# A searched table of due times replaced by ten rounds of forward and backward list scheduling

## The chip, the cores and the metric

The kernel runs on one core of a Trainium2 chip. The core has five engines that run side by side, each through its own list of instructions in order: TensorE (PE, matrix products; PEld is its weight load), VectorE (DVE), ScalarE (ACT), GpSimd (POOL) and SyncE (SP, which here only issues DMAs). They meet through semaphores: an instruction that waits holds back everything behind it on its own engine. The metric is the time of one execution in microseconds (us) on the device.

## The reference

Two layers, each an attention without softmax over positions and a gated MLP, on x of 2048 rows by 512, both with the same weights. Cut to what is computed:

```python
def A(x):                                  # 32 heads of 16
    q, k, v = split(x @ wqkv)
    pq, pk = q @ w_phi, k @ w_phi          # per head, 16 x 16
    phi_q = [softmax(pq), softmax(-pq)]    # over 16 features
    phi_k = [softmax(pk), softmax(-pk)]
    kv, z = phi_k.T @ v, sum_s phi_k       # per head, over all 2048 rows
    return (phi_q @ kv / (phi_q @ z + 1e-6)) @ wo

def B(x):
    gate, up = x @ W_gate, x @ W_up        # 512 -> 1376
    return (relu(gate) * up) @ W_down      # 1376 -> 512

for layer in range(2):
    x = x + A(layernorm(x))
    x = x + B(layernorm(x))
```

## The kernel before

The 2048 rows are 16 tiles of 128. All of x stays on the chip; the weights are loaded once. The work of a layer, per tile unless said otherwise:

- **Keys.** Mean and variance of the row (`stats`, L524, and `aggr`, L525, VectorE), the root (`ln`, L530, and `rstd`, L532, ScalarE), the scaled row (`xnA`, L535, VectorE), its transpose by a DMA that SyncE issues (L512; tiles 0 to 3 of layer one go over TensorE instead, L515). Then the products `K` (L555) and `V` (L561), four matmuls each; two exponentials of K (`ek`, L558, ScalarE), their sums (`sk`, L566, VectorE), the reciprocals (`lnk`, L569, and `rk`, L571, ScalarE), the normalised features (`phi`, L575: on GpSimd for tiles 0 to 14 of layer one, half on GpSimd and half on VectorE for tile 15, nearly all on VectorE in layer two), the copy of V (`vext`, L479, ScalarE), and the product `kvz` (L590), summed over all tiles in three PSUM banks.
- **Queries**, for four tiles at a time and a quarter of the features: the product `Q` (L627) and two exponentials `Eq` (L631, ScalarE). The weight for it is wq times w_phi, made from wq transposed out of DRAM by DMA (L487, folded at L500).
- **Read-out.** When all keys of the layer are summed and copied (`R`, L607, L614, VectorE), each tile has three packs of products `erq` (L645), two copies of each by ScalarE (L652, `DS` for the denominators and `N`), a chain on VectorE (`m`, `den`, `rden`, `w`, `pr`, `o`, L658 to L670), a transpose `oT` (DMA, or TensorE and ScalarE for the first two tiles of a layer), the product `proj` with wo (L674) and the sum into x (`resA`, L678, VectorE).
- **MLP**, in blocks of one to four tiles: statistics again, centring (`xc`, L693), a transpose `xnTB`, the products `G` and `Up` (L717), a relu and a copy by ScalarE (`rg`, L729, and `ru`, L732), their product (`hT`, L735, VectorE), the products `down` (L753), and the sum into x (`resB`, L760, VectorE). In layer two the finished tile is stored.

Nobody writes the order of these operations by hand. The code makes a list of 2,072 operations, each with its engine, its buffers, an assumed occupancy and latency, and a due time. The function `plan` then walks through the list: it keeps a clock for each engine and, at each step, takes the engine that can go first and on it, of the operations that could start within 1 ns of that moment, the one with the earliest due time. It models the few PSUM and SBUF buffers, a lock between VectorE and GpSimd (`port`), and a queue of DMAs. The order it returns is the order in which each engine's instructions are emitted. So the due times set the order on all five engines, and nothing else in the program depends on them. In the kernel before, `arrange` reads them from a table of 2,072 numbers, `DUE`, that stands in the file.

Of the kernel before, what the change touches and what calls it, by code (L numbers as in the profile page):

```python
# [148 lines left out]
def arrange(ops):  # L149
    taker = {b: o for o in ops for b in o.takes}  # L150
    last = {}
    for o in ops:
        for b in o.takes:
            if b.pool.fifo:
                if b.pool in last:
                    o.follow.append(last[b.pool])
                last[b.pool] = o
    assert len(ops) == len(DUE)
    for n, o in enumerate(ops):
        o.n, o.due = n, DUE[n]  # L160
        o.follow += {taker[b] for b in o.uses} - set(o.deps) - set(o.follow)
        for d in o.deps:
            d.then.append(o)
        for d in o.follow:
            d.behind.append(o)
    return plan(ops)
# [39 lines left out]
class K:  # L206
# [7 lines left out]
)  # L214
PHI = ["POOL"] * 15 + ["BOTH"]
BLOCKS = ((1, 1, 2, 4, 4, 2, 2), (1, 1, 2, 4, 4, 2, 1, 1))

DUE = (  # L220
    12838, 22903, 21957, 14591, 13091, 13645, 15535, 64723, 20066, 21946, 22404, 37433, 28497, 23438, 37063, 39628,
    28785, 29551, 44842, 28330, 24305, 34896, 63622, 64383, 20084, 27070, 12367, 25403, 16122, 20963, 16400, 20414,
    28622, 14745, 13296, 0, 20852, 19738, 11034, 1902, 20892, 15574, 21335, 14487, 15440, 22432, 23645, 18853, 17105,
    22553, 28873, 19773, 26092, 25340, 25787, 23828, 13120, 23528, 21785, 24083, 23090, 21952, 20538, 24815, 23457,
    25970, 23550, 31010, 25099, 23275, 18650, 19003, 26038, 17503, 25082, 25647, 15810, 16800, 15591, 12341, 14834,
    14960, 22006, 26736, 27644, 31701, 20249, 19795, 19482, 28729, 28028, 25143, 23422, 23168, 21986, 20764, 21010,
    18380, 22535, 26069, 26704, 26760, 27662, 26937, 23439, 25716, 25111, 22983, 25319, 23584, 22831, 20905, 24972,
    20900, 23792, 31557, 26979, 24090, 26712, 27328, 29633, 36593, 23721, 21790, 27888, 29989, 28308, 24211, 23690,
    16282, 27043, 28746, 63959, 20753, 24108, 22204, 20506, 28938, 31501, 16952, 23241, 24872, 26922, 26823, 26681,
    23442, 21284, 21898, 21956, 23204, 34727, 23722, 25793, 25045, 24516, 28101, 34925, 27683, 29170, 28253, 28875,  # L230
    30193, 28228, 27230, 20124, 19920, 25218, 34824, 20364, 26494, 23600, 22279, 25188, 32338, 24418, 23597, 25625,
    24807, 22909, 26881, 23790, 23537, 27214, 30398, 27170, 29691, 24862, 29838, 30880, 31272, 31170, 24090, 19394,
    24355, 27559, 28096, 28185, 27041, 16432, 19783, 20871, 21413, 25680, 24329, 22590, 23232, 28648, 34644, 25165,
    27573, 28614, 28868, 26952, 25768, 33460, 18665, 20698, 17926, 25363, 24420, 41432, 26543, 26946, 21970, 28607,
    28989, 25096, 31074, 29971, 29937, 25959, 28788, 30567, 21366, 23689, 25468, 26088, 25065, 28026, 32472, 33442,
    31477, 34059, 28202, 31806, 26064, 29854, 28369, 27149, 33755, 29216, 28180, 39321, 29625, 29410, 29759, 29949,
    30883, 29890, 21203, 25098, 24304, 21581, 23455, 24475, 31469, 24994, 27083, 22812, 27946, 25205, 43875, 15559,
    25460, 23347, 27182, 23482, 28342, 27010, 22914, 29784, 25417, 28800, 29241, 25959, 25485, 27617, 28609, 37268,
    25605, 25139, 29044, 33664, 26596, 31241, 22317, 27365, 31505, 25855, 27240, 29739, 29776, 24515, 29496, 27055,
    48013, 29990, 29010, 24738, 30465, 29653, 26383, 27215, 24572, 27986, 31540, 32648, 30111, 27816, 16563, 19041,  # L240
    9479, 23219, 25309, 26030, 26104, 29231, 28181, 27070, 27672, 28078, 20393, 17154, 22122, 19588, 25751, 27454,
    22139, 24767, 25652, 32015, 26913, 31404, 30354, 28037, 29609, 34266, 27656, 28104, 28466, 28450, 31160, 30434,
    26952, 30569, 30612, 27119, 30871, 33399, 32067, 34072, 29086, 34212, 32746, 34162, 34371, 32689, 31635, 34109,
    30452, 37680, 37561, 41767, 41154, 37244, 39966, 41520, 39034, 39714, 38939, 40611, 36774, 37121, 40048, 41493,
    40952, 40145, 35401, 33634, 20214, 31855, 33609, 22183, 27678, 29428, 20348, 24850, 30274, 21932, 28328, 31959,
    27444, 26877, 28606, 28895, 24453, 29898, 25480, 23901, 30133, 28911, 24856, 31383, 32228, 24030, 31506, 28199,
    32754, 31472, 31274, 25668, 31210, 30983, 31349, 33831, 34333, 33193, 27960, 30503, 30056, 29661, 29544, 32065,
    30471, 32168, 24516, 30101, 33395, 31799, 26788, 23122, 25970, 29642, 30372, 35556, 29123, 28474, 26295, 29799,
    27380, 29844, 29799, 26910, 29198, 22079, 25297, 29171, 32706, 31300, 31881, 33230, 30935, 33150, 30287, 28298,
    32473, 30062, 29409, 29680, 30383, 30476, 33342, 32180, 31884, 29485, 29126, 29096, 33750, 23466, 26796, 33931,  # L250
    30478, 30721, 31905, 30348, 31049, 32479, 30642, 29053, 27874, 29598, 32147, 30603, 25630, 31540, 36090, 27634,
    32676, 33746, 30843, 29434, 32969, 31529, 32324, 31334, 31554, 34777, 34212, 32334, 38155, 32871, 30137, 29960,
    27864, 27548, 35055, 34867, 30643, 30379, 32482, 31185, 33273, 31190, 30927, 29246, 28310, 31240, 38117, 29632,
    31893, 34024, 31843, 26885, 32603, 33936, 31021, 29366, 34535, 31275, 26896, 30743, 31011, 31248, 32477, 23864,
    32959, 25458, 29236, 31247, 34346, 26139, 33228, 38199, 31455, 38062, 40710, 31812, 38651, 40364, 31420, 41742,
    34183, 28837, 32652, 31832, 34298, 28327, 30341, 29521, 35561, 33294, 32671, 38050, 36251, 32854, 38333, 38562,
    31856, 42479, 47161, 29669, 28655, 35988, 32438, 29020, 34168, 29930, 35502, 32080, 31770, 41960, 44038, 32126,
    40768, 41997, 32384, 40042, 36094, 30450, 23249, 35852, 30672, 27603, 33194, 29517, 25790, 23365, 31969, 35815,
    34051, 32276, 32677, 33417, 32709, 35178, 32911, 41034, 32059, 37788, 34836, 33304, 30046, 24875, 36165, 42408,
    33005, 31288, 32714, 33009, 32695, 34948, 32971, 33157, 31154, 31289, 32065, 32216, 35950, 28322, 32715, 31866,  # L260
    34581, 38918, 33400, 32312, 34615, 33401, 30952, 29225, 33240, 29997, 32764, 35036, 31619, 31739, 35561, 28264,
    32661, 27143, 25474, 38415, 34139, 37169, 35696, 33672, 36588, 36260, 33373, 35663, 35325, 37087, 39060, 37213,
    40757, 38129, 39949, 32093, 28904, 44808, 26281, 23717, 30612, 29287, 28651, 31781, 29154, 30604, 30605, 27971,
    19455, 30444, 32192, 32972, 35192, 25843, 34053, 24821, 32438, 28904, 28598, 31101, 33142, 30192, 36853, 34142,
    31304, 36776, 38570, 34072, 34662, 27968, 31921, 30844, 33276, 30806, 28450, 28930, 33808, 35547, 33531, 35034,
    27487, 29455, 28111, 24253, 24752, 28720, 29320, 30241, 30766, 32247, 34650, 31105, 35302, 33157, 31455, 31976,
    28113, 27319, 28926, 31152, 32178, 31237, 26533, 29784, 27762, 26808, 27896, 29403, 32610, 32160, 33168, 32548,
    29999, 25348, 30314, 32356, 31798, 33774, 33234, 40285, 36802, 36151, 31849, 36427, 37365, 38953, 32525, 32074,
    32873, 35492, 32324, 29222, 29663, 29307, 38125, 39140, 38942, 35984, 32710, 33259, 30344, 38714, 38074, 33909,
    33810, 35507, 40774, 39521, 34177, 33151, 33204, 38964, 39062, 37331, 29902, 32687, 40461, 35895, 39415, 36562,  # L270
    39879, 38848, 40193, 33545, 30755, 36289, 37328, 40134, 34332, 34808, 29741, 31738, 34797, 33036, 33110, 31368,
    39810, 36739, 31632, 41406, 43305, 43018, 40166, 39122, 40506, 35174, 39940, 34497, 37182, 38991, 35093, 31782,
# [75 lines left out]
    66357, 59015, 58156, 56125, 59439, 60008, 65707, 62271, 61658, 66817, 65272, 71786, 60405, 64927, 60050, 68777,  # L348
    62597, 61141, 59298, 53316, 66598, 59726, 64329, 60736, 60887, 63694, 53405, 52936, 58957, 57884, 56732, 64533,
    52682, 65197, 59050, 66268, 61731, 62661, 60728,  # L350
)


@with_exitstack
def kernel(
# [55 lines left out]
    ops = []  # L411
# [407 lines left out]
    order = arrange(ops)  # L819
# [33 lines left out]
```

## Time and profile before

| | |
|---|---|
| median of 3 runs | 398.37 us (398.29 to 398.43) |
| the profiled execution | 398.29 us, of which 396.5 us are the span from its first to its last instruction |
| TensorE busy | 385.0 us, 97% of the span |
| VectorE, ScalarE, GpSimd busy | 267.1, 259.2, 34.2 us |
| TensorE idle, 0 to 10 us | 2.61 us |
| 10 to 40 us | 3.10 us |
| 60 to 80 us | 1.31 us |
| 110 to 120 us | 0.09 us |
| 250 to 270 us | 1.37 us |
| 390 to 396.5 us | 3.05 us |

Each idle time is the length of the stretch less TensorE's busy time in it. In all other stretches of 10 us TensorE is busy for 10.00 us. Layer one's keys and queries take the first 62 us, its read-out and the first MLP blocks lie between 62 and 130 us, layer two's keys start at 104 us in between the MLP, its read-out starts at 250 us.

How such a page is read: a row of a group gives line, engine, operation, the tiles that it writes and reads, how often, and its busy time; "idle before" is the time the engine stood still ahead of those instructions, with what ended the wait. A timeline gives start, duration, and the same names in order of time. Neighbours on VectorE and ScalarE overlap by some 0.1 us, so the cost of an instruction in a row of them is the distance of two starts, a little less than its duration.

### The profile page before, as it was taken

The page shows a single profiled execution, that of the slowest core. Times are in us where ns is not written, and L with a number is a line of the kernel's source. Part 1 is how long each engine was busy: PE and PEld are TensorE (multiplying, and loading weights), DVE is VectorE, ACT ScalarE, POOL GpSimd, SP SyncE. Part 2 cuts the span into 40 slices and gives each one's busy share as a digit, 9 for nine tenths or more (in the row PEclk, how much of TensorE's full clock was granted, in tenths as well). Part 3 has the DMA queues.
Part 4 walks back from the last instruction along what each step waited for, and adds up shares of the span by engine and source line. Part 5 has one row for each costly group of instructions (what it writes and reads, how often), then busy time and mean ns, then how long its engine had stood idle before and what let it go on. Part 6 is the DMA issues. An engine that isn't in the chain of part 4 may idle for free.

```text
span 396.5 us, 7594 instructions
## 1 busy us (share of the span) xinstructions
PE 385.0 (97%) x2819; PEld 232.2 (59%) x2819; DVE 267.1 (67%) x657; ACT 259.2 (65%) x694; POOL 34.2 (9%) x24
## 2 busy tenths in 40 slices
PE   7898998999999999999999999999999999999996
PEld 4453555886664444455666755577865445444866
DVE  5999756999999442579882467799997513423323
ACT  4888999986745566537683669998842651660622
POOL 0355970000000000000000003000000000000000
PEclk9999999999999999999999999999999999999999
DMA  6548750225314000130100100013334102001010
GB/s 213 128 125 222 163 165 1 28 56 87 74 28 91 18 0 2 26 67 15 40 16 2 26 2 0 14 28 70 76 73 93 29 0 74 8 1 54 14 41 28
DMA packets 56293, 21.78 MB, mean 55 GB/s; under 512 B 48096, under 2 KB 55232, under 8 KB 56256
## 3 DMA queue, kind: packets, MB, share of 16 engines
q1 hardware_dynamic: 55168, 20.25, 22.9%
q10 hardware_dynamic: 1088, 1.05, 0.8%
q8 instruction: 22, 0.36, 0.4%
q14 instruction: 15, 0.12, 0.1%
HBM read 7.91 MB, written 2.10 MB: 25 GB/s over the span
## 4 chain that ended last, share of the span: by engine, by line
PE 74%; DVE 12%; ACT 4%; issue 2%; DVEq 0%
PE b L717 35%; PE b L753 17%; PE b L561 5%; PE b L555 5%; PE b L674 4%; PE b L627 4%; PE q L590 3%; DVE X L678 2%; ACT Eq L631 2%; DVE bstB L524 2%; DVE pr L667 2%; PE q L645 1%; DVE o L670 1%; ACT N L652 1%; DVE m L662 1%
## 5 line engine op out<-in xcount | busy, mean ns | idle before, releaser
L717 PE MATMUL b<-xnTB,wu 128*128 128x128 bf16 (+4 forms) x660 | 89.7, 279 | 0.1
L717 PE MATMUL b<-xnTB,wg 128*128 128x128 bf16 (+5 forms) x660 | 89.3, 279 | 0.0
L729 ACT ACTIVATE gu<-b 128x512 bf16<-128x512 f32 (+4 forms) x98 | 54.6, 572 | 51.4 <-PE b L717 50.8
L735 DVE TENSOR_TENSOR hT<-gu 128x512 bf16<-128x512 bf16 (+4 forms) x98 | 37.9, 392 | 71.2 <-ACT gu L732 70.8
L753 PE MATMUL b<-wd,hT 128*128 128x512 bf16 (+2 forms) x363 | 83.2, 373 | 0.0
L732 ACT CAST gu<-b 128x512 bf16<-128x512 f32 (+3 forms) x98 | 54.3, 563 | 37.6 <-PE b L717 36.9
L717 PEld LDWEIGHTS <-wu 128*128 128x128 bf16 (+1 forms) x660 | 55.2, 100 | 25.1 <-issue 0.4
L717 PEld LDWEIGHTS <-wg 128*128 128x128 bf16 (+1 forms) x660 | 55.0, 100 | 25.4
L753 PEld LDWEIGHTS <-hT 128*128 128x128 bf16 (+1 forms) x363 | 34.8, 98 | 34.8
L575 POOL TENSOR_TENSOR phiK<-ek,sk 128x1024 bf16<-128x1024 bf16 (+1 forms) x18 | 33.5, 1878 | 211.7 <-DVE sk L566 185.1
L652 ACT CAST N<-q 128x384 bf16<-128x384 f32 (+1 forms) x96 | 48.2, 588 | 2.8 <-PE q L645 2.5
L631 ACT ACTIVATE Eq<-b 128x512 bf16<-128x512 f32 x64 | 40.4, 674 | 7.5 <-PE b L627 7.4
L566 DVE TENSOR_REDUCE sk<-ek 128x64 f32<-128x1024 bf16 x32 | 38.1, 1210 | 10.5 <-ACT ek L558 10.2
L558 ACT ACTIVATE ek<-b 128x512 bf16<-128x512 f32 x64 | 35.8, 615 | 5.3 <-PE b L555 5.1
L760 DVE SCALAR_TENSOR_TENSOR X<-b,rsB,X 128x512 bf16<-128x512 f32 (+1 forms) x33 | 23.0, 726 | 23.2 <-PE b L753 23.2
L555 PE MATMUL b<-Wk,xnTA 128*128 128x512 bf16 x128 | 32.3, 379 | 1.6 <-ACT vext L479 1.2
L674 PE MATMUL b<-wo,oT 128*128 128x512 bf16 x128 | 32.2, 379 | 1.4 <-ACT oT L479 0.8
L561 PE MATMUL b<-wv,xnTA 128*128 128x512 bf16 x128 | 32.3, 379 | 0.7 <-ACT ek L558 0.7
L627 PE MATMUL b<-xnTA,Wq 128*128 128x512 bf16 x128 | 31.5, 379 | 0.3 <-ACT Eq L631 0.3
L652 ACT COPY DS<-q 128x48 f32<-128x48 f32 (+1 forms) x96 | 25.1, 340 | 3.1 <-PE q L645 1.7
L645 PE MATMUL q<-R,Eq 128*128 128x144 bf16 x256 | 25.4, 226 | 0.6 <-ACT N L652 0.6
L645 PEld LDWEIGHTS <-Eq 128*128 128x128 bf16 x256 | 19.2, 98 | 8.2 <-issue 0.9
(63 smaller groups left out, 373.2 us busy)
## 6 DMA issues: line engine op xcount, KB each, us to landing
out_dram<-X SPq DMA_DIRECT2D x15, 128.0 KB, 1.7
X<-in_A_x_dram SPq DMA_DIRECT2D x6, 256.0 KB, 3.6
wg<-in_B_W_gate_dram SPq DMA_DIRECT2D x4, 344.0 KB, 4.3
wu<-in_B_W_up_dram SPq DMA_DIRECT2D x4, 344.0 KB, 3.9
wd<-in_B_W_down_dram SPq DMA_DIRECT2D x5, 256.0 KB, 4.1
hT<-in_A_wqkv_dram ACTq DMA_DIRECT2D x2, 256.0 KB, 3.5
X<-in_A_x_dram SPq DMA_DIRECT2D x4, 128.0 KB, 3.7
wv<-in_A_wqkv_dram ACTq DMA_DIRECT2D x2, 256.0 KB, 4.9
```

The source lines that it names most:

```text
L555: k = op("PE", mm(4, 512), due, lambda: [nc.tensor.matmul(kp.t[:], lhsT=xnTA[c][:, b, cols], rhs=Wk2[:, b, :], start=(b == 0), stop=(b == ...
L561: v = op("PE", mm(4, 512), due_v, lambda: [nc.tensor.matmul(vp.t[:], lhsT=xnTA[c][:, b, cols], rhs=wv[:, b, :], start=(b == 0), stop=(b == ...
L566: a = op("DVE", SUM16, due, lambda: nc.vector.tensor_reduce(out=sk.t[:], in_=ek.t[:].rearrange("p s (h f) -> p (s h) f", f=DH), axis=AX.X, ...
L627: q = op("PE", mm(4, 512), due(c, b), lambda b=b, qp=qp: [nc.tensor.matmul(qp.t[:], lhsT=Wq2[:, m, b * P:(b + 1) * P], rhs=xnTA[c][:, m, : ...
L631: done.append(op("ACT", act(512), due(c, b), lambda b=b, s=s, qp=qp: nc.scalar.activation(out=Eq[c][:, b, s, :], in_=qp.t[:], func=AF.Exp, ...
L645: pe.append(op("PE", mm(len(groups), GE), due, lambda ps=ps, groups=groups: [nc.tensor.matmul(ps.t[:, n * GE:(n + 1) * GE], lhsT=Eq[c][:, ...
L652: nc.scalar.copy(out=q[:, k, 0:3] if k < 2 else q[:, :, 3], in_=ps.t[:, 0:n * GE].rearrange("p (n c j) -> p n c j", n=n, j=HB)[:, :, lo:hi])
L674: a = op("PE", mm(4, 512), due + 3, lambda: [nc.tensor.matmul(yp.t[:], lhsT=oT.t[:, b, :], rhs=wo[:, b, :], start=(b == 0), stop=(b == NB ...
L717: nc.tensor.matmul(ps.t[:m, q * W:(q + 1) * W], lhsT=w[:, b, g * P:g * P + m], rhs=xT.t[:, b, 0:W], start=(b == 0), stop=(b == NB - 1))
L729: nc.scalar.activation(out=gu.t[:m, 0, lo * W:hi * W], in_=gp.t[:m, lo * W:hi * W], func=AF.Relu)
L732: nc.scalar.copy(out=gu.t[:m, 1, lo * W:hi * W], in_=up.t[:m, lo * W:hi * W])
L753: nc.tensor.matmul(yp.t[:, 0:c1 - c0], lhsT=h.t[:m, f * W + i * P:f * W + (i + 1) * P], rhs=wd[:m, f, c0:c1], start=(f == 0), stop=(f == N ...
```

## The change

The table `DUE` goes. `arrange` becomes `refine`: it starts from the due times that each operation is given where it is made (such as `K0 + KS * t` for the keys of tile t), runs `plan`, then `back`, which schedules the same operations from the end backwards and sets each one's due time to how long before the end it had to be done; it repeats that ten times and keeps the due times of the round whose plan was shortest by the assumed costs. Operations, costs, buffers and `plan` stay.

```diff
-def arrange(ops):
+def back(ops):
+    left = {o: len(o.then) + len(o.behind) for o in ops}
+    ready = dict.fromkeys(ops, 0.0)
+    clock = dict.fromkeys(HOP, 0.0)
+    open_ = {e: [o for o in ops if o.eng == e and not left[o]] for e in HOP}
+    for _ in ops:
+        best = None
+        for e, cand in open_.items():
+            if cand:
+                at = [(max(clock[e], ready[o] + o.end - o.start - o.spent), o) for o in cand]
+                first = min(t for t, o in at)
+                if best is None or first < best[0]:
+                    best = first, max((o for t, o in at if t <= first + 1), key=lambda o: (o.start, o.n))
+        t, o = best
+        clock[o.eng] = t + o.spent
+        o.due = -clock[o.eng]
...
+def refine(ops, rounds):
...
-    assert len(ops) == len(DUE)
     for n, o in enumerate(ops):
-        o.n, o.due = n, DUE[n]
+        o.n = n
...
+    best = None
+    for k in range(rounds):
+        dues = [o.due for o in ops]
+        span = max(o.end for o in plan(ops))
+        if best is None or span < best[0]:
+            best = span, dues
+        back(ops)
+    for o, due in zip(ops, best[1]):
+        o.due = due
     return plan(ops)
...
+ROUNDS = 10
-DUE = (
-    12838, 22903, 21957, 14591, 13091, 13645, 15535, 64723, 20066, 21946, 22404, 37433, 28497, 23438, 37063, 39628,
...
-)
...
-    order = arrange(ops)
+    order = refine(ops, ROUNDS)
```

The built programs hold the same instructions on each engine, in another order. Up to about 20 us the orders are the same but for neighbours. From there, with the number of the tile behind each name (for `Q` the product's, and `Eq` 2b and 2b+1 belong to `Q` b):

```
VectorE, before: xnA6 stats8 aggr5 sk3 aggr8 stats9 stats7 aggr9 xnA5 xnA8 aggr7 sk4 stats10
  stats11 xnA7 xnA9 aggr11 aggr10 sk6 xnA10 xnA11 stats12 stats13 aggr12 sk5 aggr13 sk8 xnA12
  stats15 stats14 aggr15 sk7 sk9 sk10 aggr14 xnA13 sk11 xnA14 xnA15 sk12
VectorE, after:  xnA6 stats8 stats7 aggr8 sk3 aggr7 stats9 xnA5 xnA8 aggr9 xnA7 stats10 stats11
  aggr10 sk4 xnA9 aggr11 xnA10 sk6 stats12 stats13 xnA11 sk5 aggr12 aggr13 sk8 sk7 stats14 sk9
  aggr14 stats15 aggr15 xnA12 xnA13 xnA14 sk10 sk11 xnA15 sk12
ScalarE, before: rk2 ln5 Eq1 rstd5 Eq0 lnk3 ln8 ek(4) rstd8 rk3 ek(4) ln9 Eq4 rstd9 ln7 Eq5 rstd7
  Eq2 lnk4 ek(6) rk4 ek(6) vext6 ln10 ln11 rstd10 vext4
ScalarE, after:  rk2 Eq0 Eq1 ln8 Eq2 rstd8 Eq3 ln7 lnk3 rstd7 Eq4 rk3 ln9 ek(4) rstd9 ek(4) Eq5
  ek(6) ln10 ek(6) rstd10 lnk4 vext4 rk4 ln11 vext6
TensorE, before: Q0 K4 V4 Q2 kvz2 Q1 K6 V6 kvz3 Q3 V5 K5 K8 kvz4 V8 K7 V7 K9 K10 Q4 kvz5 Q5 K11
TensorE, after:  Q0 Q1 Q2 Q3 K4 kvz2 K6 V4 V6 kvz3 K5 V5 K8 K7 V7 kvz4 K9 Q4 Q5 K10 V8 kvz5 K11
SyncE, before:   X transpose11 wu wg transpose12 wo wu wg transpose13
SyncE, after:    X wu transpose11 wg wu wu wu wg transpose12 transpose13 transpose14
```

In the read-out of layer one the packs of a tile stood apart before and stand together after, as the start shows (`erq` counts packs, three for a tile; `oT` 0 and 1, and `xnTB` 0, are the turns of the first tiles on TensorE):

```
TensorE, before: oT0 erq9 erq7 proj0 erq10 erq11 oT1 erq13 erq12 erq16 xnTB0 proj1 erq14 G0
TensorE, after:  oT0 erq7 erq8 proj0 erq9 erq10 erq11 oT1 erq12 proj1 erq13 erq14 erq15 xnTB0 erq16 G0
```

The MLP blocks go through `G` and `Up` in rising order and in pairs after, where before they were mixed; a `down` product now stands at least two matrix operations behind the last `Up` that it needs, where before it was often one.

## The prediction

> **What bounds the kernel now.** First the busy times of the page, then its slices.
>
> ```profile
> PE 385.0 (97%) x2819; PEld 232.2 (59%) x2819; DVE 267.1 (67%) x657; ACT 259.2 (65%) x694; POOL 34.2 (9%) x24
> PE   7898998999999999999999999999999999999996
> DVE  5999756999999442579882467799997513423323
> ACT  4888999986745566537683669998842651660622
> POOL 0355970000000000000000003000000000000000
> ```
>
> TensorE is the bound: it stands still for 396.5 - 385.0 = 11.5 us. Both kernels have the same 2,820 matmuls, so only these idle times can move. By stretch (the table of the section before) 2.61 us lie before 10 us and 3.05 after 390, where both orders begin and end alike; 5.87 are left: 3.10 between 10 and 40 us, 1.31 and 0.09 in the first read-out, 1.37 in the second. That caps a gain, less small waits that the tails of pipelined matmuls hide; a loss has no such cap.
>
> What makes the largest of these? The waits of 10 to 62 us by engine, for TensorE and ScalarE, then VectorE's timeline and GpSimd's.
>
> ```profile
> PE b L555 <- ACT vext L479: 1.2, 1, 1.2
> PE b L561 <- ACT ek L558: 0.7, 2, 0.5
> ...
> 26.34 0.29 ACT L530 ACTIVATE lnA<-mvA,eps 128x1 f32<-128x1 f32 x1 [1.11 <-DVE mvA L525]
> 31.05 0.48 ACT L530 ACTIVATE lnA<-mvA,eps 128x1 f32<-128x1 f32 x2 [1.61 <-DVE mvA L525]
> ...
> 23.90 2.32 DVE L535 TENSOR_SCALAR xn<-X,mvA,rsA 128x512 bf16<-128x512 bf16 x2
> 28.53 2.33 DVE L535 TENSOR_SCALAR xn<-X,mvA,rsA 128x512 bf16<-128x512 bf16 x2
> 32.04 0.72 DVE L535 TENSOR_SCALAR xn<-X,mvA,rsA 128x512 bf16<-128x512 bf16 x2
> ...
> 24.06 2.01 POOL L575 TENSOR_TENSOR phiK<-ek,sk 128x1024 bf16<-128x1024 bf16 x1 [0.72 <-ACT sk L571]
> 28.61 2.10 POOL L575 TENSOR_TENSOR phiK<-ek,sk 128x1024 bf16<-128x1024 bf16 x1 [2.54 <-PE b L627]
> ```
>
> The reader is to see one chain. Two scalings take 0.72 us together at 32.04, but 2.32 and 2.33 where GpSimd's multiply began 24.06 and 28.61, just ahead of the second scaling of each pair: each time 1.6 us are lost until the multiply is over. Behind it on VectorE waits `aggr`, for that `ln` waits (1.11, 1.61), behind `ln` on ScalarE stand `ek` and `vext`, and for their PSUM banks TensorE waits: 0.46 + 1.24 + 0.28 = 1.98 us between 29 and 36 us.
>
> The Trainium skill states the same: SBUF — State Buffer, Who interferes with whom, has the pair of SBUF ports that VectorE and GpSimd share as an exclusive lock, and whoever comes second blocks until the first is done. It speaks against this change at one place, below.
>
> **The change part by part.**
>
> *Same work, same ends.* Instructions and their durations stay: 0. The first 20 us differ by the order of two loads and four folds of equal size, the last 10 us by one 0.44 us product: 0, within 0.3 either way.
>
> *Stage of keys, 20 to 62 us.* I step the new order from rk2, at 21.07 in both. Distances of starts in the rows: an exponential 0.47, `ln` 0.19, `rstd` 0.09, `lnk` 0.15, `sk` 1.10, `stats` 0.60, `aggr` 0.09, a scaling 0.32. ScalarE after: `Eq0` at 21.65 (product `Q0` starts at 20.56 and takes 1.03), then up to rk3 five `Eq`, two `ln`, two `rstd`, one `lnk`: 2.35 + 0.38 + 0.18 + 0.15 = 3.1, so rk3 at 24.75 and the multiply of tile 3 at about 25.1 instead of 24.06. VectorE after: from 20.8 two `stats`, `aggr`, `sk3`, `aggr`, `stats`: 1.2 + 0.1 + 1.1 + 0.1 + 0.6 = 3.1, so xnA5, xnA8, `aggr`, xnA7 run from 23.9 to 25.0, the last starting 0.5 us ahead of the multiply. The next pair, xnA9 and xnA10, comes behind two `stats`, `aggr` and sk4, which waits for the second `ek` of tile 4 (at 25.7, done 26.3): 27.5 and 28.0. The multiply of tile 3 is over by 27.1; that of tile 4 needs rk4, at about 28.5, and starts at 28.9. Both collisions are gone, with 0.4 to 0.9 us to spare. Tiles 7 to 10 reach their transposes 0.8 to 2.5 us earlier, and the 1.98 us on TensorE go: -2.0.
>
> What is late next: tiles 12, 13 and 14 are now scaled in a row, at VectorE's work of 37 to 38 us. From 36 us GpSimd multiplies with almost no gap (rows of 5.75 and 5.78 us for three each). Behind the three stand sk10, sk11 and the scaling of tile 15, whose transpose feeds `K15`, 40.1 us of matmul work in, against 41.4 before. That wait is not in the trace; nearest rows: in the same stretch before, the scalings of tiles 13, 14 and 15 took
>
> ```profile
> 41.93 1.41 DVE L535 TENSOR_SCALAR xn<-X,mvA,rsA 128x512 bf16<-128x512 bf16 x1
> 44.72 0.89 DVE L535 TENSOR_SCALAR xn<-X,mvA,rsA 128x512 bf16<-128x512 bf16 x2
> ```
>
> so one of them lost 1.0 and the pair 0.2. Lower end: nothing is blocked for long, K15 on time, 0. Upper: all three lose 1.6 as at 24.06, 4.9 on VectorE, and tile 15 meets another multiply; K15 is then 2.4 to 4.4 us late. I take 0.8, between one loss of 1.0 and one of 1.6 with some cover left, as the row in the same stretch is nearest. By the skill's rule alone each of the three would be blocked for up to a whole multiply, 1.93 us, so up to 5.8; the sum would then be near the upper end.
>
> *Queues.* Five weight loads now stand ahead of the transpose of tile 12 on SyncE: 5 x 0.6 = 3.0 us of issuing from about 35 us, over by the time that tile's scaling ends (37.8 or later): 0. Its data, behind 1.7 MB, may land after 4.5 us instead of 2.4 (longest and shortest of the transposes of 15 to 47 us): up to 2.1, covered because K12 stands 5.7 us of matmul work behind K11; if that cover went, +2. On GpSimd the multiplies keep their order but for tiles 7 and 8. No wait is added elsewhere; the waits for DMA lanes stay one of eight back.
>
> *First read-out.* Before, from the first `erq` (61.70) to G0 (71.31) pass 9.6 us for 7.6 us of matmuls: 2.0 lost. After, worked out with the same rows: proj0 has only two packs between it and oT0, and their copies stand ahead of the copy it needs: 0.9; proj1 one pack: 0.7; G0 one pack, behind copies of three: 0.8. Together 2.4: +0.4. Later, VectorE is full from 72 to 124 us (page: 9 in all slices), and its work ahead of what a product needs, set against the matmul work ahead of that product, comes shortest at `kvz` of layer two's second tile: 0 to 0.8 late. I take 0.2; sum +0.6. Ends: -0.3 if ScalarE is ahead after an earlier stage end, +2.0 if proj2, 3, 4 and 10 (0.4 to 0.6 us of cover each) slip too.
>
> *Second read-out.* Before, 249.9 to 262.0: 12.1 us for 9.8 of matmuls, 2.3 lost. After, the copy of oT2 stands behind copies of packs that come later (0.37 + 0.37 + 0.26), but the turn of the next tile has more work ahead: 2.5. +0.2, between -0.6 and +1.0.
>
> *MLP and layer two's keys, 71 to 250 us and 262 to 390.* TensorE never waits there now but for 0.09. After, the down products have more cover, at least 1.7 us for a chain of relu, copy and multiply of 1.1; thinnest is `K30`, with 0.2 us. 0; if those covers went, 0.3 to 0.5 each.
>
> Sum: -2.0 + 0.8 + 0.6 + 0.2 = -0.4 us on the profiled execution: 398.29 - 0.4 = 397.9. That execution lies 0.08 under the median, 398.37; I forecast 397.9. About 0.2% (0.8 us) is what a measurement of this kernel can tell from no change.
>
> **The rivals.**
>
> *Kept gain.* The three scalings find gaps and the read-outs are as before: -2.0 alone, 396.3. For it: at 45.20 a scaling took 0.40 between multiplies. Against: GpSimd's stretches of three without a gap.
>
> *Slower: the scalings of tiles 12 to 14 blocked one after the other.* Place: VectorE near 38 us. Price: K15 late by 2.4 to 4.4 instead of 0.8, with 0.8 for the read-outs: 398.3 - 2.0 + 3.4 + 0.8 = 400.5. It decides as soon as GpSimd starts a multiply before two of the three. For it: that stretch is 95% busy (9.51 of 10 us from 40 to 50).
>
> *Slower: packs in threes.* Three packs use all three banks, so each next three wait for six copies in order on ScalarE; the upper ends of both read-outs, +2.0 and +1.0, with -2.0 + 0.8: 400.1. Against: ScalarE has a slack from 82 us on.
>
> That the order did not change is excluded by the built programs.
>
> **How the numbers follow.** Forecast 0.42, own range 397.0 to 398.9 (0.14 under 397.57, 0.26 within, 0.02 above 399.17); kept gain 0.20, faster; blocked scalings 0.25 and packs 0.13, slower. Faster 0.34, same 0.26, slower 0.40. Range 396.0 to 401.4: from a little below the kept gain to the later half of the blocked scalings, leaving out about 1 in 10 on each side.
>
> **What would show it.** Right: near 24 and 28 us no scaling of 2.0 us, no `ln` wait above 1 us, TensorE over 9.5 busy in 30 to 40 us, first `erq` near 60.5 instead of 61.7; scalings above 1 us near 38 us; G0 about 10 us after the first `erq`. Wrong, if the multiply of tile 3 starts before 24.7, if K15 waits more than 2 us, or if TensorE waits between 130 and 240 us, where I have nothing.

## The result

The changed kernel takes 400.58 us (median of 6 runs, 399.36 to 400.88), the kernel before 398.36 (6 runs, 398.29 to 399.44): a ratio of 1.0044, 95% interval 1.0025 to 1.0062. It is slower by 0.4%. The forecast was 397.9 us, 0.1% under the kernel before, with chances of 0.34 for faster, 0.26 for the same and 0.40 for slower.

Part of this is not in the order. An execution of either kernel draws one of two levels, 1.1 to 1.3 us apart, by its TensorE clock in the first 12 us (last section); the kernel before drew the lower one in 5 of these 6 runs, the changed kernel in 2. On the lower level it takes 399.36 and 399.50 against 398.29 to 398.43, so the order costs 1.0 to 1.1 us. From here on a time "at full clock" is the median of the executions whose mean clock is 0.999 or 1.0, and differences are taken to the kernel before at full clock in the same comparison (398.35 to 398.52).

The profiled execution of the changed kernel took 399.36 us, with a span of 397.6. Its page, busy times and slices:

```profile
PE 384.3 (97%) x2819; PEld 231.8 (58%) x2819; DVE 268.1 (67%) x657; ACT 259.5 (65%) x694; POOL 33.6 (8%) x24
PE   6899898999999999999999999999999999999996
DVE  5999767999997262578884357799979723222322
ACT  4899789967764656627582849997656566606042
POOL 0348670000000000000000002000000000000000
```

The fourth slice of TensorE, low before (30 to 40 us), is full, and the fifth, which was full, is not. The stretches (columns: stretch, length, then busy time and instructions of PE, PEld, DVE, ACT and POOL, granted clock, DMA share, GB/s) of the kernel before, then of the changed kernel:

```profile
20.00:30.00 10.00, 9.54 (x63) 5.10 (x62) 10.00 (x17) 7.92 (x26) 5.33 (x3) 1.00 0.53 134
30.00:40.00 10.00, 8.48 (x51) 4.08 (x49) 9.58 (x18) 8.95 (x28) 5.20 (x4) 1.00 0.80 220
40.00:50.00 10.00, 10.00 (x71) 5.51 (x70) 6.59 (x8) 10.00 (x32) 9.51 (x6) 1.00 0.77 161
50.00:62.00 12.00, 12.00 (x95) 6.99 (x94) 6.37 (x10) 10.84 (x26) 6.66 (x4) 1.00 0.42 128
```

```profile
20.00:30.00 10.00, 10.00 (x65) 5.30 (x65) 9.36 (x20) 9.68 (x32) 4.96 (x3) 1.00 0.70 157
30.00:40.00 10.00, 10.00 (x66) 5.27 (x65) 9.84 (x16) 10.00 (x34) 8.63 (x6) 1.00 0.81 221
40.00:50.00 10.00, 8.85 (x60) 4.67 (x59) 7.38 (x6) 7.24 (x19) 5.79 (x3) 1.00 0.87 174
50.00:62.00 12.00, 11.02 (x92) 6.60 (x91) 7.57 (x11) 10.38 (x27) 7.17 (x4) 1.00 0.35 111
```

From 20 to 40 us TensorE was idle for 0.46 + 1.52 = 1.98 us before; now it is busy all the time. But 1.15 us are idle in 40 to 50 and 0.98 in 50 to 62, where the kernel before had TensorE busy all the time, and the first `erq` stands at 61.62 instead of 61.70: of the 2 us almost nothing is left. What ended TensorE's waits from 16 to 62 us:

```profile
PE b L532 <- ACT vext L384: 1.0, 1, 1.0
PE q L495 <- ACT sk L476: 1.0, 1, 1.0
```

and behind it, from the timelines (start, duration, then line, tiles and number): VectorE's scalings L440 and sums L471, GpSimd's multiplies L480, ScalarE's `lnk` L474 and `vext` L384:

```profile
23.82 0.72 DVE L440 TENSOR_SCALAR xn<-X,mvA,rsA 128x512 bf16<-128x512 bf16 x2
27.48 0.41 DVE L440 TENSOR_SCALAR xn<-X,mvA,rsA 128x512 bf16<-128x512 bf16 x1
37.79 4.29 DVE L440 TENSOR_SCALAR xn<-X,mvA,rsA 128x512 bf16<-128x512 bf16 x3
42.00 2.33 DVE L471 TENSOR_REDUCE sk<-ek 128x64 f32<-128x1024 bf16 x2
44.25 2.02 DVE L440 TENSOR_SCALAR xn<-X,mvA,rsA 128x512 bf16<-128x512 bf16 x1
...
25.02 1.93 POOL L480 TENSOR_TENSOR phiK<-ek,sk 128x1024 bf16<-128x1024 bf16 x1 [1.72 <-PE b L460]
36.12 5.80 POOL L480 TENSOR_TENSOR phiK<-ek,sk 128x1024 bf16<-128x1024 bf16 x3 [0.24 <-ACT rsA L437]
44.20 3.86 POOL L480 TENSOR_TENSOR phiK<-ek,sk 128x1024 bf16<-128x1024 bf16 x2 [2.27 <-ACT sk L476]
...
43.24 0.26 ACT L474 ACTIVATE sk<-sk 128x64 f32<-128x64 f32 x1 [2.76 <-DVE sk L471]
43.40 0.57 ACT L384 CAST vext<-b 128x512 bf16<-128x512 f32 x1
```

The two collisions of before are gone: the pair of scalings at 23.82 takes its 0.72 us, the one at 27.48 its 0.41, and the multiply of tile 3 starts at 25.02. A third one has come. At 37.79 the scalings of tiles 12, 13 and 14 take 4.29 us together, the second and third 2.02 and 2.01 each, under a gapless row of multiplies (36.12, 5.80 us for three). Behind them on VectorE stands sk10, whose exponentials had been ready since 38.50. It starts at 42.00; ScalarE has waited 2.76 us for it at 43.24, and behind that `lnk` stand the copies of V that TensorE waits for at 44.02. The second wait ends at 55.04: its row names a reciprocal on ScalarE, but the product there reads the features of tile 13, and GpSimd's multiply of that tile ends at 54.99. GpSimd had stood still for 3.11 us until 51.17, waiting for a reciprocal on ScalarE.

### The profile page after: what moved, and what is told of

It reads as the page before. It is cut to its first block, busy times and chain, and to the rows that moved or that the text cites. A ratio compares the mean times of both kernels' runs of the same rounds, so it can differ in the third digit from the quotient of the medians.

```text
span 397.6 us, 7614 instructions
## 1 busy us (share of the span) xinstructions
PE 384.3 (97%) x2819; PEld 231.8 (58%) x2819; DVE 268.1 (67%) x657; ACT 259.5 (65%) x694; POOL 33.6 (8%) x24
## 4 chain that ended last, share of the span: by engine, by line
PE 78%; DVE 3%; ACT 2%; issue 0%; DVEq 0%; ACTq 0%
PE b L622 39%; PE b L658 19%; PE b L579 6%; PE b L460 3%; PE b L466 3%; PE q L550 3%; PE b L532 2%; PE q L495 2%; DVE pr L572 1%; ACT Eq L536 1%; ACT N L557 1%; DVE X L583 0%; DVE m L567 0%; DVE o L575 0%; PE b L420 0%
## 5 line engine op out<-in xcount | busy, mean ns | idle before, releaser
L634 ACT ACTIVATE gu<-b 128x512 bf16<-128x512 f32 (+2 forms) x98 | 55.1, 573 | 65.5 <-PE b L622 62.9
L622 PE MATMUL b<-xnTB,wg 128*128 128x128 bf16 (+2 forms) x660 | 91.8, 279 | 0.1
L622 PE MATMUL b<-xnTB,wu 128*128 128x128 bf16 (+2 forms) x660 | 91.8, 280 | 0.0
L640 DVE TENSOR_TENSOR hT<-gu 128x512 bf16<-128x512 bf16 (+2 forms) x98 | 38.1, 394 | 73.9 <-ACT gu L637 73.6
L637 ACT CAST gu<-b 128x512 bf16<-128x512 f32 (+2 forms) x98 | 54.3, 563 | 25.7 <-PE b L622 25.0
L622 PEld LDWEIGHTS <-wg 128*128 128x128 bf16 x660 | 55.3, 100 | 26.3 <-issue 0.3
L622 PEld LDWEIGHTS <-wu 128*128 128x128 bf16 x660 | 55.1, 100 | 23.7
L480 POOL TENSOR_TENSOR phiK<-ek,sk 128x1024 bf16<-128x1024 bf16 (+1 forms) x18 | 32.9, 1846 | 212.8 <-DVE phiK L480 184.9
L557 ACT CAST N<-q 128x384 bf16<-128x384 f32 (+1 forms) x96 | 46.8, 552 | 0.0
L471 DVE TENSOR_REDUCE sk<-ek 128x64 f32<-128x1024 bf16 x32 | 38.4, 1210 | 8.1 <-ACT ek L463 8.0
L557 ACT COPY DS<-q 128x48 f32<-128x48 f32 (+1 forms) x96 | 22.0, 292 | 6.0 <-PE q L550 4.7
L550 PE MATMUL q<-R,Eq 128*128 128x144 bf16 x256 | 24.4, 226 | 1.0 <-ACT N L557 0.8
```

The source lines that it names most:

```text
L471: a = op("DVE", SUM16, due, lambda: nc.vector.tensor_reduce(out=sk.t[:], in_=ek.t[:].rearrange("p s (h f) -> p (s h) f", f=DH), axis=AX.X, ...
L550: pe.append(op("PE", mm(len(groups), GE), due, lambda ps=ps, groups=groups: [nc.tensor.matmul(ps.t[:, n * GE:(n + 1) * GE], lhsT=Eq[c][:, ...
L557: nc.scalar.copy(out=q[:, k, 0:3] if k < 2 else q[:, :, 3], in_=ps.t[:, 0:n * GE].rearrange("p (n c j) -> p n c j", n=n, j=HB)[:, :, lo:hi])
L622: nc.tensor.matmul(ps.t[:m, q * W:(q + 1) * W], lhsT=w[:, b, g * P:g * P + m], rhs=xT.t[:, b, 0:W], start=(b == 0), stop=(b == NB - 1))
L634: nc.scalar.activation(out=gu.t[:m, 0, lo * W:hi * W], in_=gp.t[:m, lo * W:hi * W], func=AF.Relu)
L637: nc.scalar.copy(out=gu.t[:m, 1, lo * W:hi * W], in_=up.t[:m, lo * W:hi * W])
```

## The experiments

In the experiments each engine's order is written out as a list of operations instead of being planned, and buffers are given by the rule of `plan`; so single instructions can be moved, and the two orders can be joined where both have finished the same operations on every engine. Lines of the code stand in other places there: the scaling is L596, `sk` L627, `phi` L636, `vext` and the turned copies L540, `Q`'s copies L713, centring L754.

All results, with the number of executions at full clock. The ratio takes the executions of both levels; the last column compares at full clock alone.

| kernel | ratio to before, 95% interval | at full clock (of all) | against before there |
|---|---|---|---|
| s1 | 0.9989 (0.9973 to 1.0006) | 398.21 us (8 of 12) | -0.14 |
| s2 | 1.0013 (1.0000 to 1.0025) | 399.21 (7 of 12) | +0.86 |
| s3 | 0.9999 (0.9986 to 1.0011) | 398.64 (7 of 12) | +0.29 |
| x1 | 0.9971 (0.9957 to 0.9985) | 397.43 (6 of 12) | -0.92 |
| x4 | 1.0177 (1.0155 to 1.0200) | none of 5: 404.58 to 407.05 | |
| y1 | 0.9945 (0.9927 to 0.9963) | 396.05 (4 of 6) | -2.32 |
| y2 | 0.9939 (0.9924 to 0.9954) | 396.32 (5 of 5) | -2.05 |
| b12 | 0.9994 (0.9983 to 1.0006) | 398.77 (12 of 12) | +0.42 |
| x3 | 1.0037 (1.0024 to 1.0051) | 399.81 (7 of 11) | +1.44 |
| x5 | 1.0046 (1.0030 to 1.0063) | 400.31 (5 of 8) | +1.96 |
| va | 1.0023 (1.0007 to 1.0039) | 399.10 (6 of 12) | +0.72 |
| vb | 0.9983 (0.9970 to 0.9996) | 397.83 (7 of 12) | -0.55 |
| z2 | 0.9999 (0.9985 to 1.0012) | 398.36 (5 of 12) | -0.08 |
| z3 | 1.0038 (1.0021 to 1.0055) | 399.89 (7 of 12) | +1.45 |
| vz | 1.0033 (1.0017 to 1.0049) | 399.84 (7 of 12) | +1.32 |

A few executions stand some 2 us above their level, at full clock 399.52 in x1, 401.77 in z3 and 401.70 in vz; why is not known. The table has medians.

### Where the time is lost: s1, s2, s3

```diff
  per engine:            to first erq   to layer 2's last keys   rest
  kernel before             before            before             before
+ s1                        after             before             before
+ s2                        before            after              before
+ s3                        before            before             after
```

> The order of the kernel after up to the first read-out matmul on every engine, the order of the kernel before from there on. Theory A (the difference is the sum of what the trace shows stretch by stretch: keys stage -0.14, first read-out +1.0, second +0.3): 398.1 to 398.3 us, ratio to before 0.9995, the same. Theory B (the time is lost in the keys stage, and the later stages only pass it on): 399.3 to 399.6, ratio 1.003. Theory C (half of the difference is not in the order but in a lower clock that an execution can draw): single executions at two levels about 1.2 us apart here and in the kernel before as well, whichever stretch is taken.

> The order before up to the first read-out matmul, the order after from there to the last key tiles of layer 2, the order before for the rest. Theory A: +1.0 of the first read-out, 399.3 us, ratio 1.0025, with the waits of TensorE for ScalarE's copies near 67, 69 and 72 us. Theory B: nothing, 398.3.

> The order before up to the last key tiles of layer 2, the order after from the second read-out on. Theory A: +0.3, 398.6 us, ratio 1.0008. Theory B: nothing, 398.3. If the second level of the time lies in this stretch of the order (Theory C turned into one of order), most executions stand at 399.5.

Measured: -0.14, +0.86 and +0.29; their sum, +1.01, is the difference of the two kernels at full clock. Theory A holds and Theory B falls: the keys stage ends level, and the loss lies in the two read-outs. Theory C holds as well: both levels came in every one of these kernels. The waits of TensorE from 60 to 80 us, s1 and then s2:

```profile
PE b L735 <- ACT oT L540: 0.6, 1, 0.6
PE q L706 <- ACT N L713: 0.6, 1, 0.6
```

```profile
PE b L735 <- ACT oT L540: 1.6, 2, 1.0
PE q L706 <- ACT N L713: 0.9, 2, 0.5
```

The order after waits for two turned copies (`oT` of both tiles 0 and 1) instead of one, and for two copies of read-out groups instead of one: 1.3 us more in such rows.

### What eats the gain of the keys stage: x1

```diff
  VectorE: sk7 stats14 sk9 aggr14 stats15 aggr15 xnA12
-   xnA13 xnA14 sk10 sk11 xnA15 sk12
+   sk10 xnA13 sk11 xnA14 xnA15 sk12
```

> The kernel after, with two sums over key features moved on VectorE: the sum of tile 10 ahead of the scaling of tile 13 and the sum of tile 11 ahead of the scaling of tile 14, which wait for GpSimd's multiplies (2.02 and 2.01 us); nothing else moved. Theory D (the blocked scalings cost the stage what it had won, through the two sums, ScalarE's 2.76 us wait for the first of them and the value copies behind it): the waits of TensorE of 1.04 and 0.2 us near 44 and 45 go, and the 0.98 near 55 shrinks, together -1.2 to -2.2: 397.2 to 398.2 where the kernel after profiled 399.36. Theory E (the transposes of tiles 12 to 14, landing after 6.1, 4.6 and 3.1 us behind five weight loads, hold the stage, and the sums are hidden behind them): less than 0.4 won, TensorE waits for the transpose of tile 12 instead.

Measured: 397.43 at full clock, 2.0 under the changed kernel (399.36 and 399.50), at the upper end of what Theory D expects and far outside Theory E. VectorE's rows:

```profile
38.75 0.48 DVE L596 TENSOR_SCALAR xn<-X,mvA,rsA 128x512 bf16<-128x512 bf16 x1
39.63 1.22 DVE L627 TENSOR_REDUCE sk<-ek 128x64 f32<-128x1024 bf16 x1 [0.40 <-ACT ek L619]
40.77 0.40 DVE L596 TENSOR_SCALAR xn<-X,mvA,rsA 128x512 bf16<-128x512 bf16 x1
41.51 1.22 DVE L627 TENSOR_REDUCE sk<-ek 128x64 f32<-128x1024 bf16 x1 [0.34 <-ACT rsA L593]
42.64 2.40 DVE L596 TENSOR_SCALAR xn<-X,mvA,rsA 128x512 bf16<-128x512 bf16 x2
```

sk10 starts 0.9 us after the start of the scaling of tile 12 instead of 4.2 (this execution runs 1.1 us later from the start), the scalings of tiles 13 and 14 take 0.40 and 0.46 where they took 2.02 and 2.01, and only the last scaling is still blocked. ScalarE's wait of 2.76 us and both of TensorE's waits of 1.0 are gone; GpSimd's multiplies run five in a row without a gap. Moving the sums also freed two of the scalings, so x1 alone does not part the two. The changed kernel's own trace does: no row there has `K12` to `K15` waiting for the transposes that the scalings feed, and its first wait leads through `vext` and `lnk` back to sk10. So it was the two sums that carried the loss to TensorE.

### Do the late transposes matter: x4

```diff
  SyncE: X wu transpose11
-   wg wu wu wu wg transpose12 transpose13 transpose14
+   transpose12 transpose13 transpose14 wg wu wu wu wg
    wo wo wo transpose15 wo wd ...
```

> The kernel after, with the five weight loads that were issued at 34.1 to 36.2 us, ahead of the transpose of tile 12, put behind the transpose of tile 14 on SyncE's queue; nothing else moved. Theory D: the transposes land 2.4 to 3 us after issue instead of 6.1, 4.6 and 3.1, but TensorE does not wait for them: within 0.3 us of the kernel after on each level (399.4 and 400.6). Theory E: 0.4 to 2 us won.

Measured: all five executions at 404.58 to 407.05 us, 5 to 7.6 over the changed kernel at full clock, which neither theory had. The transposes of tiles 12 to 14 do land after 2.4 us each, and it brings nothing: K12 starts at 45.15, as in the changed kernel. But the loads now stand ahead of the transpose of tile 15. It is issued at 47.95 instead of 46.30 and lands after 5.7 us instead of 2.4, and K15 waits:

```profile
PE b L616 <- DMA xnTA<-xn: 4.5, 1, 4.5
PE b L688 <- ACT vext L540: 1.1, 1, 1.1
```

The second row is the 1.0 us at 44 us, hardly changed. So in the changed kernel the loads ahead of tile 12 cost nothing because K12 had cover. Without cover a transpose that was issued 1.65 us later and landed 3.3 us later, behind eight loads of 2.1 MB together, cost TensorE 4.5 us. Behind that wait the granted clock stands at 0.50 once more, from 54.5 us on, for 3.41 us.

### A kernel that keeps the gain: y1 and y2

```diff
  per engine:            to first erq       rest
+ y1                     x1 (after + sums)  before
+ y2: y1, and the warm-up of 12 matmuls instead of 8
-        start=True, stop=True) for _ in range(8)], [c_z], [wps], name="warm")
+        start=True, stop=True) for _ in range(12)], [c_z], [wps], name="warm")
```

> Keys stage in the order of the kernel after with the two sums moved (as in x1), everything from the first read-out on in the order of the kernel before. Theory A and D together: x1 stands at 397.4 on its lower level, less the 0.86 of the first read-out and the 0.29 of the second: 396.2 on the lower level, 397.4 on the upper, about 0.5% under the kernel before on the same level. Rival: the read-outs only pass on what the keys stage wins (they wait for ScalarE, which is still at the queries' exponentials): 397.2 on the lower level.

> As y1, with 12 matmuls of the warm-up in place of 8. Theory H (the upper level is the record's window of 3.41 us at half clock after TensorE's idle at 6.1 to 8.5 us: 1.76 us busy in the window before it in x1, against 1.92 in the kernel after, which kept its clock; which window falls there is drawn by the start): four more matmuls fill it, no execution on the upper level, all within 0.4 us of 396.2. Rival (the level is set by something else, or four more matmuls delay the first turns): both levels as in y1, or all about 0.5 to 0.9 longer.

Measured: y1 takes 396.05 at full clock (396.02 to 396.13; 397.37 and 397.50 on the upper level), 2.32 us under the kernel before: ratio 0.9945 (0.9927 to 0.9963). The parts add up as A and D have it, and what the keys stage wins goes through to the end. It beats both kernels; the rival (397.2) falls. y2 stood on the lower level five times of five, between 396.01 and 396.46.

### The first read-out: x3, x5, z3

```diff
# x3, from the kernel after
  VectorE: resA0
-   pr2 stats16 m3 o2 aggr16 den3 xc0
+   stats16 aggr16 xc0 pr2 m3 o2 den3
  TensorE: erq12
-   proj1 erq13 erq14 erq15 xnTB0 erq16 G0 erq17
+   xnTB0 proj1 erq13 erq14 erq15 G0 erq16 erq17
  ScalarE: (copy of xnTB0 ahead of the last copy of erq12 instead of behind those of erq13)
# x5, from x3
  TensorE:
-   G0 erq16 erq17 erq18 erq19 Up0
+   G0 Up0 erq16 erq17 erq18 erq19
  ScalarE: (rg0 and ru0 ahead of the copies of erq16)
# z3, from x3
  ScalarE: (second copy of erq15 ahead of the first of erq16)
```

> The kernel after, in the first read-out alone: on VectorE the statistics and the centring of tile 0 ahead of the product of tile 2, on TensorE and ScalarE the transpose of the centred tile 0 and its copy earlier (ahead of the product with wo of tile 1; ahead of the copies of the fifth pack's numerators), one read-out matmul group behind the first gate block. Theory F (the order put tile 2's division ahead of tile 0's centring, so the first gate block waits): G0 starts 0.5 to 0.9 earlier and the kernel takes 398.6 to 399.0 on the lower level against 399.4 to 399.5 of the kernel after. Rival G (ScalarE is saturated there and what is put ahead only delays something else as long): within 0.2 of the kernel after.

> As x3, and besides the first gate and up products (G0, Up0) ahead of the read-out groups 16 to 19 on TensorE, with their two evictions ahead of the copies of groups 16 and later on ScalarE: in the kernel before, two gate products stand between the read-out groups at this place, in the kernel after one. Theory J (TensorE asks for read-out groups faster than ScalarE copies them out, and the kernel before lets ScalarE catch up behind products that need no copy from the read-out): the waits of 0.68 and 0.19 us that x3 had at groups 18 and 19 go, 398.8 to 399.1 on the lower level, 0.4 to 0.6 under the kernel after. Rival G (ScalarE has that much work ahead of the first block in either order): the wait comes back at a later group or product, 399.4 to 399.9.

> x3 with one copy moved on ScalarE: the second copy of read-out group 15 ahead of the first of group 16, which in x3 waited for a matmul group that had been put behind the first gate product. Theory V with that flaw: the waits of 0.68 and 0.19 us at groups 18 and 19 go or halve, 399.0 to 399.4 on the lower level, under the kernel after (399.43). Rival: they stay, 399.7 to 399.9 as x3.

Measured: none wins. x3 stands 0.4 over the changed kernel, x5 0.9, z3 0.5. Theories F and J fall, and z3's version of V with them. Rival G says rightly that nothing is won, but had x3 within 0.2 of the changed kernel and x5 at 399.9 at most; only z3's rival has its number right. In x3 the first gate product does start 0.7 us earlier (71.95 instead of 72.66), but the groups behind it wait:

```profile
PE b L735 <- ACT oT L540: 1.0, 1, 1.0
PE q L706 <- ACT N L713: 0.9, 2, 0.5
PE b L576 <- DVE xn L754: 0.7, 1, 0.7
```

The sum, 2.6 us, is no less than what the changed kernel has there (2.1 in such rows, 2.5 in s2). x3 had a flaw: the first copy of group 16 stood ahead of the second of group 15, which then waited for a matmul moved behind the gate product. z3 mends it, the waits at groups 18 and 19 fall from 0.68 + 0.19 to 0.36 + 0.30, and the end does not move.

### Is it ScalarE: va, vb, vz

```diff
  def queries(c, due, xT, after):
+     n = 8 if c == 3 and not after else 512
...
-     out=Eq[c][:, b, s, :], in_=qp.t[:], func=AF.Exp, scale=1.0 - 2.0 * s
+     out=Eq[c][:, b, s, 0:n], in_=qp.t[:, 0:n], func=AF.Exp, scale=1.0 - 2.0 * s
# va: kernel after; vb: s1; vz: z3
```

> The kernel after, with most of the query exponentials of the last 512 queries of layer 1 left out: each of these eight instructions on ScalarE does 8 columns in place of 512, and the rest of their tile is ones, written by GpSimd at the start. Nothing is moved. This takes about 0.4 us off ScalarE eight times between 63 and 80 us, five of them ahead of the first gate block (about 2.0 us). Theory S (ScalarE, busy 4.00, 3.97 and 4.00 of each 4 us from 64 to 76 us, sets TensorE's waits at the first read-out): the waits of 3.2 us there shrink by 1.0 to 2.0, 397.4 to 398.4 on the lower level against 399.43. Theory L (the waits are the latency of the chain product, copy, division, transpose, in whatever order ScalarE works): less than 0.5 won, 398.9 or more.

> The same left out of s1 (the order of the kernel after up to the first read-out, of the kernel before from there on), which stands at 398.2. Theory S: its waits of 2.1 us there shrink too, and what the two orders of the read-out differ by (0.86 of the 1.2 us between s1 and the kernel after) shrinks with ScalarE's load: 396.8 to 397.5, and va less vb under 0.8. Theory L: less than 0.5 won, and va less vb stays at 1.2.

> z3 (VectorE centres tile 0 ahead of tile 2's product, and the first gate block comes earlier) with the same query exponentials left out as in va (about 0.4 us off ScalarE eight times between 63 and 80 us). va stands at 399.1 and z3 at 399.8 on the lower level. Theory W (two limits one behind the other: with VectorE's order mended ScalarE's copies hold the next groups, with ScalarE relieved VectorE's order holds the first block): both together win 1.0 to 1.5 against the kernel after, 397.9 to 398.4. Rival L (the latency of the chain and the runs of groups on TensorE, whoever does them): 398.9 to 399.5, no better than va.

Measured: va wins 0.3, vb 0.4, and va less vb stays at 1.27 (before: 399.43 less 398.21, 1.22). vz takes 399.84, no better than z3. Theories S and W fall. Theory L keeps its numbers in va and vb; its 399.5 at most for vz is passed by 0.3. ScalarE, full in the changed kernel, has air in va. Two stretches of the one and then of the other (fourth busy time: ScalarE; the profiled execution of va runs 1.2 us later from its start):

```profile
64.00:68.00 4.00, 3.00 (x26) 1.84 (x25) 3.66 (x11) 4.00 (x16) 0.00 (x0) 1.00 0.00 0
68.00:72.00 4.00, 3.00 (x32) 2.10 (x31) 3.97 (x14) 3.97 (x16) 0.00 (x0) 1.00 0.05 10
```

```profile
64.00:68.00 4.00, 3.27 (x30) 2.01 (x28) 3.52 (x11) 3.37 (x16) 0.00 (x0) 1.00 0.00 0
68.00:72.00 4.00, 3.25 (x28) 2.00 (x29) 3.93 (x14) 3.66 (x14) 0.00 (x0) 1.00 0.01 2
```

By the distances of its starts, TensorE's five waits there shrink from 3.1 to 2.7 us and no more. VectorE, next to it, stays at 3.93 of 4.00.

### Is it VectorE's order: z2

```diff
# z2, from y1
  VectorE: pr1
-   o1 resA0 stats16 m3 aggr16 den3 xc0
+   m2 o1 den2 rden2 w2 resA0 pr2 stats16 m3 o2 aggr16 den3 xc0
  TensorE: oT0 erq9 erq7
-   proj0
+   erq8 proj0
  ScalarE: (the two copies of erq8 behind those of erq7)
```

> y1 with tile 2's read-out ahead of the first block, as the kernel after has it: on VectorE the division, product and sum of tile 2 (the rows of the kernel after: m, den, rden, w, pr and o, 1.6 us of issue time) stand between tile 1's product and tile 0's centring, and the third read-out group of tile 2 with its two copies stands with the others; nothing else is moved. Theory V (VectorE paces the first read-out, and each of its instructions ahead of tile 0's centring moves the first gate block): centring and G0 come 0.8 to 1.2 later than in y1, 396.8 to 397.2 on the lower level against 396.1. Rival L2 (the rest of the order, the runs of read-out groups behind one another on TensorE, makes the difference): within 0.3 of 396.1.

Measured: 398.36 at full clock, 2.3 over y1, more than Theory V expects. The centring of tile 0 in y1, in z2, and what TensorE waited for in z2 (60 to 80 us):

```profile
67.42 0.35 DVE L754 TENSOR_SCALAR xn<-X,mvB 128x512 bf16<-128x512 bf16 x1
```

```profile
65.94 0.22 DVE L719 TENSOR_TENSOR m<-DS 128x64 f32<-128x64 f32 x1 [0.64 <-ACT DS L713]
69.64 0.35 DVE L754 TENSOR_SCALAR xn<-X,mvB 128x512 bf16<-128x512 bf16 x1
```

```profile
PE b L576 <- DVE xn L754: 1.7, 1, 1.7
PE q L706 <- ACT DS L713: 1.1, 1, 1.1
```

Six instructions of tile 2 ahead of tile 0's centring move it 2.2 us back: 0.14 because this execution reaches the first `erq` that much later, 0.64 of waiting, and the rest for themselves. The 0.64 comes because the third group of tile 2 comes late for a PSUM bank (the 1.1 us) and all of VectorE stands behind its `m`. TensorE pays 1.7 of it in one wait. This shows the price of that order in a kernel that otherwise has the order of before; x3 and z3 show that taking the two largest of the six (`pr` and `o`) away from there does not mend the kernel after. Which single pieces of its order carry the 0.86 us of s2, and by which engine, stays open.

### The two levels: b12

```diff
# b12, from the kernel before
-        start=True, stop=True) for _ in range(8)], [c_z], [wps], name="warm")
+        start=True, stop=True) for _ in range(12)], [c_z], [wps], name="warm")
```

> The kernel before, with 12 matmuls of the warm-up in place of 8; nothing else. Theory H (the upper level is a window of 3.41 us at half clock behind TensorE's idle at 6.1 to 8.5 us): all executions on the lower level, 398.1 to 398.7, while the kernel before draws both levels, 398.3 and 399.6. Rival: both levels here too, or one level that is later by what the four matmuls take, 0.9 to 1.7 us at the clocks seen.

Measured: all 12 executions at a clock of 0.999 or 1.0, where the kernel before beside it had 9 of 19 at 0.995 or 0.996. Theory H holds for the clock. For the time it holds in part: 398.26 to 399.23, up to 0.9 us over the kernel before at full clock. Against the mixture of the kernel before the ratio is 0.9994 (0.9983 to 1.0006), which is nothing.

## Why the prediction was wrong

**Same work, same ends (0): right.** Both kernels and all the splices agree with it.

**Keys stage, the collisions (-2.0): right.** Tile 3's multiply at 25.02 (25.1 forecast), the scalings at 23.82, 27.48 and 28.49 (23.9, 27.5 and 28.0), TensorE at 10.00 of 10 from 20 to 40 us. y1 shows that it goes through to the end.

**Keys stage, the scalings of tiles 12 to 14 (+0.8): wrong, and this is the first step that failed.** That place, and that they could all be blocked, stood in the text, with the row "41.93 1.41" preferred over the 2.32 us pairs as the nearest, and the 0.8 lies under both of the losses, 1.0 and 1.6, that it was said to lie between. Of the four scalings of tiles 12 to 15, three took 2.02, 2.01 and 2.02. The error in kind is larger than that in size: the step named "sk10, sk11 and the scaling of tile 15" as standing behind, and then followed only the scaling, to K15. K15 came without a wait. The sums were priced at nothing, although `ek` of tile 10 was ready long before, and `lnk`, `vext` and the Q products stood behind them on two more engines. The step cost 1.9 instead of 0.8: forecast for the stage -1.2, measured -0.14 (s1), with the -2.0 in it. The rival with blocked scalings was right in its place and wrong in its way (K15 late by 2.4 to 4.4) and so too dear: 400.5 on a level where the kernel takes 399.4. That it lies near the median of 400.58 is an accident of the two levels. The page SBUF — State Buffer of the Trainium skill (Who interferes with whom), which lets each be blocked for up to a whole multiply, was nearer than the row: 2.02 less 0.40 is 1.6 us for each.

**Queues (0): right, and the bound of +2 too small.** The transpose of tile 12 landed after 6.1 us, not 4.5, and K12 did not wait for it. With cover gone and the transpose issued later too, as in x4, it is 4.5 us and a lower clock on top.

**First read-out (+0.6): right in sign, a little small; the cause not shown.** s2 has +0.86, within the bounds of -0.3 and +2.0. The three waits were named right (proj0, proj1, G0: forecast 0.9, 0.7, 0.8; measured in the rows of TensorE's starts 1.15, 0.50 and 0.30, besides 0.54 and 0.61 at groups 12 and 16, which were not forecast). They were put down to ScalarE's copies. That is what the chain of waits names; with five exponentials cut by about 0.4 us each on ScalarE ahead of G0, va won only 0.3 us. The rival of packs in threes was not tried by itself; what comes nearest is z2, where the third pack of tile 2 waited 1.1 us for its bank.

**Second read-out (+0.2): right** (s3: +0.29). **MLP and layer two's keys (0): right**: TensorE is busy for 170.00 of the 170 us from 80 to 250 and 126.00 of the 126 from 264 to 390.

Together the steps gave -0.4; at full clock the order gives +1.0 to +1.1, and 1.1 of the 1.4 to 1.5 between them is the one step in the keys stage. The rest of the +2.2 between the medians is the level that each execution drew, which the prediction did not have: its three runs of the kernel before lay within 0.14 us, all on one level, and it took 0.8 us for what can be told from no change.

Of "what would show it", four signs came out as right for the gain (no long scaling near 24 and 28, no long wait of `ln`, TensorE full in 30 to 40, nothing between 130 and 240 us), and the one that counted did not: the first `erq` at 61.62 instead of 60.5; G0 then came 11.0 us behind it, not 10. Scalings above 1 us near 38 were named there, with too little behind them. Of the three signs of being wrong none came: none of them watched the sums.

## What to carry to other kernels

When an instruction may be held up, list everything that stands behind it on its own engine, and price each of these by who waits for it; the costly one need not be the one that the instruction itself feeds. A large reordering can be taken apart by joining the two orders where they have done the same work: three runs told that the stage which gained and lost came out even, and one moved pair of sums, with the read-outs of before, made it the fastest kernel here (y1, 0.55% under the kernel before). And where several engines are full in one stretch, the engine that a wait names need not be the one to relieve; take its work away and look before writing it down as the cause.

## What was not expected of the hardware

**A half-clock window drawn by the start.** The clock's record of the profiled executions changes only at the ends of windows of 3.41 us, whose place against the start differs from execution to execution: the first full-clock window began anywhere from 4.00 to 7.37 us in 17 profiles. In x1, va, z3 and vz the next window was granted half the clock again. Stretch 8.0 to 11.4 us in x1 and, beside it, in s1 (granted clock: the last column but two):

```profile
8.00:11.40 3.40, 2.79 (x19) 2.14 (x20) 3.03 (x6) 1.57 (x4) 0.00 (x0) 0.50 0.22 64
```

```profile
8.00:11.40 3.40, 2.80 (x27) 1.81 (x28) 3.40 (x7) 2.11 (x5) 0.00 (x0) 1.00 0.30 79
```

TensorE's busy time in the first full-clock window, the one ahead of that, was 1.74, 1.55, 1.70 and 1.68 us of 3.41 in these four, and 1.82 to 2.57 in the 13 that kept the clock; upwards, windows with 2.60 us or less gave no full clock and those with 2.64 or more did. Busy time alone is no threshold: later windows with as little, 1.54 us at 47.7 in x4 and 1.73 at 43.7 in vz, kept the clock. In this kernel the window that covers TensorE's idle time from about 7 to 8.5 us decides, and it costs 1.1 to 1.3 us. In 133 executions of the kernel before, beside the experiments, 75 stood on the upper level. TensorE: Matmul & The Clock Gate of the Trainium skill (Part 1) has the free-running window of this length, and puts the way down behind an idle window; in the four profiles here a window that was half busy was enough.

**Transposes by DMA behind loads.** A transpose of one tile took 2.4 us from issue to landing in x4, with no load issued in the 5 us ahead of it. In the changed kernel it took 6.1 behind five loads of 344 KB each (1.7 MB) issued in the 4 us ahead of it, and then 4.6 and 3.1 for the next two.
